# Another order for the attention steps and for the end of the last chunk in a one-core attention and expert kernel

## The chip, the cores and the metric

The kernel runs on one core of a Trainium2 chip. The core has a matrix engine (TensorE: PE for its matmuls, PEld for its weight loads), a vector engine (VectorE, DVE), a scalar engine (ScalarE, ACT), a general engine (GpSimd, POOL) and an engine that here only issues DMAs (SyncE, SP). Each of them takes its instructions strictly in the order in which they were written. They meet through semaphores. The metric is the device time of one execution in microseconds; lower is better.

## The reference

Three parts follow each other. The first is attention for 4 batches and 8 heads over 512 local and 32 global positions: local queries see the global keys and a band of keys at a distance of at most 32, global queries see everything.

```python
s_ll = np.where(np.abs(pos[:, None] - pos[None, :]) <= 32, s_ll, -1e9)
out_l = np.matmul(sm(np.concatenate([s_lg, s_ll], -1)), np.concatenate([v_g, v_l], 2))
out_g = np.matmul(sm(scale * np.matmul(q_g, k_all.transpose(0, 1, 3, 2))), v_all)
```

Its 2176 token rows of 512 go to 8 experts. `logits = x @ w_gate` are sorted over all tokens and experts, and each token goes to the expert of its largest logit that still has room (272 places each). Each expert computes `relu(x @ w1[e]) @ w2[e]` with 1024 hidden columns. The third part is dense: `h = x @ w_in` with 2048 hidden columns, a rational function `g = P(h) / (Q(|h|) + 1e-6)` of each element, and `g @ w_out`. Everything is computed in an accuracy close to float32; a product in the later parts is therefore three matmuls on high and low parts.

## The kernel before, in words

**The order is written by a planner.** Every piece of work is a Python generator that yields what it needs: an engine and a modelled duration (`yield "PE", 0.36`), an event, a buffer of a ring, or a float, which is a delay. `Flow.run` (L165 and on) asks which step could start first by the modelled clocks and writes that step's instructions next. The durations decide only the order; on the chip the semaphores decide the time. There are two planners: one for attention, one for all that follows.

**Attention.** A unit is 128 queries of one batch, all heads: 16 units, with a unit for the global queries of each batch between them. For a unit, PE computes scores (L589 adds the mask, L599 the products), VectorE takes the extreme of each row (`mx`, L614), ScalarE the exponentials (`A`, L299), PE transposes them (L632), PE multiplies by the values (`av`, L655), VectorE scales by the sums (`rs`, L663 and L664; `xs`, L666). SP then stores `xs` to DRAM, PE transposes it (L684), ScalarE or VectorE copies it (`XT`, L299), PE multiplies by the gate (L699), a copy goes to `lgT`, PE adds four quarters (L708) and VectorE copies 8 columns to `LG` (L710). These last five steps are `logits`. Before the units of a batch, keys are turned (`kr` to `KT`: PE L493, copies L299 or L306) and queries as well (`qr` to `QB`: L513, L299 or L308). Whole rows of keys and values for the windows are put together by DMAs (`VW<-vr`) and by copies of the global values on GpSimd (`VW<-vg`, L465). A copy marked `CPY` goes to ScalarE or VectorE, as the planner finds.

Beside that, 24 of 32 pieces of the third part's weights come in as 64-bit numbers in `stg` buffers (6 of them) and are turned into float32: one operation on ScalarE (L277) and three on VectorE (L278, L279, L280).

**Routing and experts.** When the last `LG` is there, a search on VectorE (L999 and on) finds the rows of the first expert; later searches lie beside matmuls. Experts run one after the other (L1250 to L1252).

**The third part** runs in 8 chunks of token blocks of 128: seven chunks of two blocks and the last one of three. `firsts` is the first layer (L1250 to L1252, into a `tq` bank, of which there are 2), `chain` the rational function on ScalarE and VectorE (L1626 to L1666; the step L1638 gives the bank back), `seconds` the second layer (L1255 to L1257, into one bank for each block). The last chunk has 16 steps. A step is 12 matmuls of the first layer and 9 of the second, 3 for each block. `store` copies a finished block on ScalarE (L1709) and scatters its rows by an indirect DMA from GpSimd (L1714). Which of `firsts` and `seconds` goes first is a matter of ranks: `seconds` has the lower rank, by 0.1, until `firsts` has reached the last chunk (`front["d"] >= E - 1`), and a higher one from there.

Of the kernel before, what the change touches and what calls it, by code (L numbers as in the profile page):

```python
# [2 lines left out]

# [28 lines left out]
FL, FM, SR = 0.45, 0.7, 0.1  # L32
WT = 5
PATIENCE = {"DVE": 0.3, "PE": 0.15, "ACT": 0.2, "POOL": 0.5}
NL = 8
LGPAD, RCPAD = 96, 160
LAG = 0.5
LAND = (5.0, 3.3, 2.3)
DRAWN = (4.5, 4.0, 3.0)


REBIAS = 2.0 ** -112
# [2 lines left out]
class Event:  # L45


    def __init__(self, n=1):
        self.n, self.at, self.waiters, self.ring = n, [], [], None
# [27 lines left out]
class Flow:  # L77
# [5 lines left out]

    SAME = {"PE": 0.0, "DVE": 0.14, "ACT": 0.08, "POOL": 0.1}

    def __init__(self, fill=None):
        self.clock, self.asks, self.now, self.fill = {}, [], [(0.0, "PE")], fill

    def lag(self, src, dst):
        return self.SAME.get(src, 0.0) if src == dst else 0.2  # L90
# [80 lines left out]
    def run(self, patience):  # L171
        while self.asks:
            best = {}
            for p in self.asks:
                r = p[1]() if callable(p[1]) else p[1]
                t, e, d = min((max([self.free(e)] + [t + self.lag(s, e) for t, s in p[2]]) + sum(less), e, d)
                              for e, d, *less in p[3])
                best.setdefault(e, []).append((t - (e == "DVE" and len(p[3]) > 1) * BIAS, r, p, d))
            pick = None
            for e, c in best.items():  # L180
                t0 = min(x[0] for x in c)
                wait = patience.get(e, 0.0)
                wait = wait() if callable(wait) else wait
                x = min((x for x in c if x[0] <= t0 + wait), key=lambda x: (x[1], x[0]))
                if pick is None or x[0] < pick[0]:
                    pick, self.engine = x, e
            t, _, p, d = pick
            e = self.engine
            if e == "PE" and self.fill is not None:
                self.fill(t - self.clock.get(e, 0.0))  # L190
            self.asks.remove(p)
            self.clock[e] = t + d
            p[2] = [(t + d, e)]
            self._on(p)
# [7 lines left out]
def moe_kernel(ctx: ExitStack, tc: tile.TileContext, q_l, k_l, v_l, q_g, k_g, v_g, w_gate, w1, w2,  # L202
# [81 lines left out]
    with ExitStack() as actx:  # L284
# [6 lines left out]

        ORD = [2 * (hh % 4) + hh // 4 for hh in range(H)]
        kraw, qraw, vraw, vgr = {}, {}, {}, {}
        flow = Flow()
        V = nc.vector
        CPY = [("ACT", 0.48), ("DVE", 0.6, BIAS)]

# [341 lines left out]
        def values(b, u, rank, at, sm, m, turned):  # L639
            yield turned  # L640
            yield vw_in[b, u // 2]
            if rank:
                yield valued[rank - 1]
            av = yield av_s
            flow.fire(valued[rank])
            pv = bank("av", 1)
            for n in range(4):
                yield "PE", 0.38
                w = win(4 * u + n)
                vw = VW[b, w // (NW // 2)][:, w % (NW // 2)]  # L650
                for hg in range(2):
                    c0 = (2 * n + hg) * D
                    for j in range(4):
                        h = ORD[4 * hg + j]
                        nc.tensor.matmul(pv[32 * j:32 * j + 32, c0:c0 + D], at[0][:, hg, n, 32 * j:32 * j + 32],  # L655
                                         vw[:, h * D:(h + 1) * D], start=True, stop=True)
            flow.fire(at[1])
            flow.fire(vw_used[b, u // 2])
            x = yield xs_s
            xs = work.tile([128, 4, 2 * D], F32, name="xs", bufs=2)  # L660
            yield "DVE", 0.2
            rs = few.tile([128, 8], F32, name="rs", bufs=3)
            V.tensor_scalar(rs, sm.rearrange("p a b -> p (a b)"), 1e-9, None, op0=OP.add)  # L663
            V.reciprocal(rs, rs)  # L664
            yield "DVE", 0.6
            V.tensor_tensor(xs.rearrange("p n (a d) -> p (n a) d", a=2), pv.rearrange("p (a d) -> p a d", d=D),  # L666
                            rs[:, :, None].to_broadcast([128, 8, D]), op=OP.mult)
            flow.fire(av)
            flow.fire(m)
            xs_free = Event(5)  # L670
            flow.go(after(xs_free, x), 0)

            def stores():
                for j in range(4):
                    yield "SP", 0.475
                    dma(dram(xd, (b * S + SG + u * 128) * DM + j * 128, [[DM, W], [W * DM, 4], [1, 128]]),
                        xs[32 * j:32 * j + 32], xs_free, 0.267)

            flow.go(stores(), rank + ST)
            tx = yield tx_s  # L680
            px = bank("tx", 1)
            yield "PE", 0.5
            for n in range(4):
                nc.tensor.transpose(px[:, n * 128:(n + 1) * 128], xs[:, n], identf)  # L684
            flow.fire(xs_free)
            xt = yield xt_s
            XT = work.tile([128, KC, 128], F32, name="XT", bufs=2)
            yield CPY
            copy(XT.rearrange("p j (n q) -> p n j q", n=4), px.rearrange("p (n j q) -> p n j q", n=4, j=4))
            flow.fire(tx)  # L690
            yield from logits(XT, 4 * b + u)
            flow.fire(xt)

        def logits(XT, c):
            tx = yield tx_s
            p = bank("tx", 1)
            yield "PE", 0.36
            for j in range(KC):
                nc.tensor.matmul(p[32 * j:32 * j + 32, :128], wg[:, j], XT[:, j], start=True, stop=True)  # L699
            yield [("ACT", 0.2), ("DVE", 0.2, BIAS)]  # L700
            lgT = work.tile([128, 128], F32, name="lgT", bufs=2)
            copy(lgT, p[:, :128])
            flow.fire(tx)

            tx = yield tx_s
            p = bank("tx", 1)
            yield "PE", 0.3
            tail_pe[:] = [nc.tensor.matmul(p[:, :E], lgT, sel, start=True, stop=True)]  # L708
            yield "DVE", 0.08
            V.tensor_copy(LG[:, c], p[:, :E])  # L710
            flow.fire(tx)
# [960 lines left out]
    def seconds():  # L1672
        for c in range(E):
            T, FW = shape(c)
            ng = T // 128
            for i in range(NSTEP[c]):
                yield g_done[c][i]
                gh, gl, slots = gs.pop((c, i))
                if i == 0:
# [4 lines left out]
                for w in range(FW):  # L1684
# [3 lines left out]
                    for g in range(ng):  # L1688
# [5 lines left out]
                        if f == FFC - 1:  # L1694
                            flow.go(store(c, g), 0.7)
                flow.fire(slots)

    ixs = {}

# [42 lines left out]
    with tc.manual_schedule(engines={ET.PE, ET.Activation, ET.DVE, ET.Pool}), tc.issue_after(tail[-1].ins), tc.issue_after(tail_pe[0].ins):  # L1742
        for gen, rank in ((router(), pace), (high(), 5), (last_pieces(), late), (low_pe(), 5), (low(V, "DVE", 0.6), late), (gather(), 0.5), (loads(), 1), (splits(), 1.5),
                          (experts(), lambda: 2 + front["e"]), (firsts(), lambda: 2 + front["d"]),
                          (seconds(), lambda: 2 + front["d"] + (SR if front["d"] >= E - 1 else -0.1))):
            flow.go(gen, rank)
        flow.run({**PATIENCE, "PE": lambda: PATIENCE["PE"] if xs_ else 0.55})

# [30 lines left out]
```

## Time and profile before

| | us |
|---|---|
| median of 3 runs | 876.4 |
| lowest of the 3 | 875.96 |
| highest of the 3 | 2771.55 |
| the profiled execution | 868.81 |
| its span, first to last instruction | 867.0 |

1.8 us of the profiled execution lie around its span. It is 7.6 us shorter than the median. The page gives busy times, the chain of work that ended last, and groups of instructions; the trace behind it can be asked for a stretch, an engine or a line. Times in it are counted from the span's start. An instruction's row has its start, its length, and in brackets the idle time of its engine before it with what ended that. Attention lies between 0 and 180 us, the first routing between 180 and 237, experts and chunks between 237 and 786, and from 786 on the last chunk is computed.

### The profile page before, as it was taken

What the parts mean: (1) busy time and instruction counts of PE and PEld (TensorE: products, weight loads), DVE (VectorE), ACT (ScalarE), POOL (GpSimd) and SP (SyncE); (2) the same over time, 40 slices, a digit from 0 to 9 for tenths busy, and PEclk for the clock granted to TensorE, in tenths of its full rate; (3) what the DMA queues carried; (4) which work ended last, traced back from release to release, by engine and by line L of the source; (5) the groups of instructions that cost most, each with busy time, mean ns of one, the idle gap of its engine ahead of it and who ended that gap; (6) DMA issues with size and microseconds to landing.
All of it is one profiled execution on the core that took longest, in us unless ns stands there. A gap on an engine that the chain in (4) does not pass through costs nothing.

```text
span 867.0 us, 21692 instructions
## 1 busy us (share of the span) xinstructions
PE 815.3 (94%) x8532; PEld 715.9 (83%) x8532; DVE 709.6 (82%) x1647; ACT 500.1 (58%) x1135; POOL 254.8 (29%) x223
## 2 busy tenths in 40 slices
PE   8988777889799999999999999999999999999997
PEld 5765555667599899989989999999999999998995
DVE  3577677688789999989989989999886867668985
ACT  5777485788355446644554564554465555555763
POOL 5511111000252323424233442424344243330001
PEclk9999897899899999999999999999999999999999
DMA  9989897234452212321321232132123132300000
GB/s 236 252 217 283 223 281 223 90 98 125 132 151 83 62 48 64 108 72 42 96 87 49 62 98 74 50 94 90 50 63 111 48 97 68 93 26 13 12 1 38
DMA packets 130543, 89.08 MB, mean 103 GB/s; under 512 B 28840, under 2 KB 119464, under 8 KB 130440
## 3 DMA queue, kind: packets, MB, share of 16 engines
q1 hardware_dynamic: 126632, 76.92, 30.9%
q0 software_dynamic: 3280, 10.75, 3.8%
q8 instruction: 67, 1.10, 0.5%
q14 instruction: 36, 0.29, 0.1%
q10 hardware_dynamic: 528, 0.02, 0.0%
HBM read 70.02 MB, written 8.92 MB: 91 GB/s over the span
## 4 chain that ended last, share of the span: by engine, by line
PE 65%; DVE 14%; issue 10%; ACT 5%; DMA 2%; POOL 2%; SPq 1%; DVEq 0%; POOLq 0%; ACTq 0%
PE sc L1250 6%; PE sc L1252 6%; PE sc L1251 6%; PE tq L1250 6%; PE tq L1251 6%; PE tq L1252 6%; PE sc L1257 5%; PE sc L1255 5%; PE sc L1256 5%; PE av L1025 2%; SPq L393 1%; PE sc L599 1%; PE av L655 1%; DVE wide_a L1021 1%; PE tq L632 1%
## 5 line engine op out<-in xcount | busy, mean ns | idle before, releaser
L1495 POOL TENSOR_TENSOR wlo<-rows,whi 128x512 fp32r<-128x512 f32 x120 | 167.6, 1399 | 333.0 <-ACT whi L1486 324.0
L1250 PE MATMUL tq<-yr,wh 128*128 128x256 f32 (+1 forms) x512 | 148.9, 291 | 1.5 <-DVE p L1638 1.5
L1252 PE MATMUL tq<-yr,ws 128*128 128x256 f32 (+1 forms) x512 | 148.0, 289 | 0.0
L1251 PE MATMUL tq<-yr,wh 128*128 128x256 f32 (+1 forms) x512 | 147.9, 289 | 0.0
L1250 PEld LDWEIGHTS tq<-yr,wh 128*128 128x128 f32 x512 | 96.9, 189 | 3.3 <-issue 2.2
L1255 PE MATMUL sc<-wh,t 128*128 128x512 f32 x248 | 99.4, 401 | 0.0
L1257 PE MATMUL sc<-wh,t 128*128 128x512 f32 x248 | 98.4, 397 | 0.8 <-DVE t L1666 0.8
L1251 PEld LDWEIGHTS tq<-yr,wh 128*128 128x128 f32 x512 | 97.0, 189 | 0.8
L1256 PE MATMUL sc<-ws,t 128*128 128x512 f32 x248 | 97.3, 392 | 0.0
L1252 PEld LDWEIGHTS tq<-yr,ws 128*128 128x128 f32 x512 | 97.0, 189 | 0.0
L1486 ACT ACTIVATE whi<-rows 128x512 fp32r<-128x512 f32 x120 | 75.0, 628 | 16.5 <-PE sc L1251 12.9
L1530 ACT ACTIVATE hh<-sc 128x272 fp32r<-128x272 f32 x64 | 25.4, 396 | 87.0 <-PE sc L1252 86.7
L1626 ACT ACTIVATE t<-tq,coef 128x512 f32<-128x512 f32 (+1 forms) x67 | 44.8, 668 | 52.2 <-PE tq L1252 40.7
L1250 PE MATMUL sc<-xhi,whi 128*128 128x272 f32 x240 | 73.5, 306 | 0.0
L1250 PE MATMUL sc<-hh,whi 128*128 128x272 f32 x240 | 70.8, 295 | 0.0
L1252 PE MATMUL sc<-xhi,wlo 128*128 128x272 f32 x240 | 69.9, 291 | 0.5 <-POOL wlo L1495 0.3
L1251 PE MATMUL sc<-xlo,whi 128*128 128x272 f32 x240 | 69.6, 290 | 0.0
L1251 PE MATMUL sc<-hl,whi 128*128 128x272 f32 x240 | 69.6, 290 | 0.0
L1252 PE MATMUL sc<-hh,wlo 128*128 128x272 f32 x240 | 69.3, 289 | 0.0
L1644 DVE SCALAR_TENSOR_TENSOR t<-t,b 128x512 f32<-128x512 f32 (+1 forms) x67 | 52.1, 778 | 20.1 <-ACT t L1628 19.9
L1647 ACT ACTIVATE t<-t,cq 128x512 f32<-128x512 f32 (+1 forms) x67 | 47.3, 706 | 23.4 <-DVE t L1644 23.0
L1257 PEld LDWEIGHTS sc<-wh,t 128*128 128x128 f32 x248 | 46.6, 188 | 15.0 <-DVE t L1666 4.8
(307 smaller groups left out, 2143.1 us busy)
## 6 DMA issues: line engine op xcount, KB each, us to landing
rows<-in_moe_w_dram SPq DMA_DIRECT2D x128, 256.0 KB, 2.8
stg<-in_moe_w_in_dram SPq DMA_DIRECT2D x16, 512.0 KB, 4.0
stg<-in_moe_w_out_dram SPq DMA_DIRECT2D x16, 512.0 KB, 6.6
VW<-vr SPq DMA_DIRECT2D x18, 256.0 KB, 6.2
kr<-in_k_l_dram SPq DMA_DIRECT2D x8, 512.0 KB, 5.7
qr<-in_q_l_dram SPq DMA_DIRECT2D x8, 512.0 KB
vr<-in_v_l_dram SPq DMA_DIRECT2D x16, 256.0 KB, 4.7
xd<-xs SPq DMA_DIRECT2D x64, 64.0 KB, 3.5
```

What stands on the lines that cost most here:

```text
L1250: nc.tensor.matmul(ps, whi, xhi, start=first, stop=False)
L1251: nc.tensor.matmul(ps, whi, xlo, start=False, stop=False)
L1252: nc.tensor.matmul(ps, wlo, xhi, start=False, stop=last)
L1255: nc.tensor.matmul(ps, ghi, whi, start=first, stop=False)
L1256: nc.tensor.matmul(ps, ghi, wlo, start=False, stop=False)
L1257: nc.tensor.matmul(ps, glo, whi, start=False, stop=last)
L1486: nc.scalar.activation(hi, raw, AF.Copy)
L1495: (V if alt else nc.gpsimd).tensor_tensor(lo, raw, hi.bitcast(F32), op=OP.subtract)
L1530: nc.scalar.activation(hh, ph[:, :CAP], AF.Relu)
L1626: nc.scalar.activation(q, ph, AF.Abs, scale=b0)
L1644: V.scalar_tensor_tensor(q, r, b1, q, op0=OP.mult, op1=OP.add)
L1647: nc.scalar.activation(r, q, AF.Ln, bias=cq)
```

## The change

Four things are altered.

- In the attention planner each modelled duration is multiplied by a number between 0.97 and 1.03, drawn from a generator with a fixed seed (31). The order is thus a fixed one again, but another.
- `logits` yields a delay of 0.7 us, in the model only, ahead of each of its three requests, for all units but those of the last three ranks. It does this ahead of taking a `tx` bank.
- `seconds` takes the higher rank already from `front["d"] >= E - 1.2`, which is within the last chunk but one.
- The last two steps of the last chunk's second layer are written block by block: both steps of block 0 and its store, then block 1, then block 2. Before, all blocks of step 14 came ahead of those of step 15.

No instruction is added or taken away. Three copies into `KT` go from ScalarE to VectorE (one from `kgT`, two from `sc`); that is the only change in the numbers of instructions on an engine.

```diff
+VARY = (31, 0.03)
+SLACK = 0.7
-    def __init__(self, fill=None):
-        self.clock, self.asks, self.now, self.fill = {}, [], [(0.0, "PE")], fill
+    def __init__(self, fill=None, vary=None):
+        self.clock, self.asks, self.now, self.fill, self.vary = {}, [], [(0.0, "PE")], fill, vary
...
             self.asks.remove(p)
+            if self.vary is not None:
+                d *= 1 + self.vary.uniform(-VARY[1], VARY[1])
             self.clock[e] = t + d
...
-        flow = Flow()
+        flow = Flow(vary=random.Random(VARY[0]))
...
-            yield from logits(XT, 4 * b + u)
+            yield from logits(XT, 4 * b + u, SLACK * (rank < 5 * B - 3))
             flow.fire(xt)
 
-        def logits(XT, c):
+        def logits(XT, c, late=0.0):
+            yield late
             tx = yield tx_s
             p = bank("tx", 1)
             yield "PE", 0.36
...
+            yield late
             tx = yield tx_s
             p = bank("tx", 1)
             yield "PE", 0.3
             tail_pe[:] = [nc.tensor.matmul(p[:, :E], lgT, sel, start=True, stop=True)]
+            yield late
             yield "DVE", 0.08
...
-            for i in range(NSTEP[c]):
+            pair = NSTEP[c] - 2 * (c == E - 1)
+            for i in range(pair):
...
+            if pair == NSTEP[c]:
+                continue
+            both = []
+            for i in (pair, pair + 1):
+                yield g_done[c][i]
+                both.append((i, *gs.pop((c, i))))
+            for g in range(ng):
+                o = slice(g * 128, g * 128 + 128)
+                for f, gh, gl, _ in both:
+                    yield "PE", mmt(512, 3)
+                    mm3t(accs[c][g], gh[:, o], gl[:, o], *wo(f), False, f == FFC - 1)
+                flow.go(store(c, g), 0.7)
+            for x in both:
+                flow.fire(x[3])
...
-                          (seconds(), lambda: 2 + front["d"] + (SR if front["d"] >= E - 1 else -0.1))):
+                          (seconds(), lambda: 2 + front["d"] + (SR if front["d"] >= E - 1.2 else -0.1))):
```

Lines of the changed kernel are 5 to 8 higher in attention and 8 higher in the chunks (L666 is L671 there, L710 is L718, L1257 is L1265). Between the end of attention and the last steps of the last chunk but one, every engine's order is the same as before. Three places follow.

The first is VectorE in the third batch of attention, at 91 us of the trace. `stg_1372` and the like are pieces of weights; `av` and `xs` belong to a unit, `mx` to the next one. Before:

```order
L710 COPY LG<-tx 128x8
L614 TENSOR_REDUCE mx<-sc 128x4 x2
L663 TENSOR_SCALAR rs<-sm 128x8
L664 RECIPROCAL rs<-rs 128x8
L279 SCALAR_TENSOR_TENSOR ws<-stg_1372,ws 128x512
L666 TENSOR_TENSOR xs<-av,rs 128x512
L280 SCALAR_TENSOR_TENSOR ws<-stg_1372,ws 128x512
L306 COPY KT<-sc 128x4x4x32 x2
```

Now:

```order
L619 TENSOR_REDUCE mx<-sc 128x4 x2
L668 TENSOR_SCALAR rs<-sm 128x8
L669 RECIPROCAL rs<-rs 128x8
L671 TENSOR_TENSOR xs<-av,rs 128x512
L718 COPY LG<-tx 128x8
L311 COPY KT<-sc 128x4x4x32
L283 TENSOR_SCALAR ws<-stg_1561 128x512
L284 SCALAR_TENSOR_TENSOR ws<-stg_1561,ws 128x512
L285 SCALAR_TENSOR_TENSOR ws<-stg_1561,ws 128x512
L311 COPY KT<-sc 128x4x4x32
```

The copy of logits and the piece's operation no longer stand ahead of `xs`; the pieces have moved behind it.

The second is VectorE at the end of attention, down to the last two copies of logits, small set-up operations of the routing apart. Of the two `LG` in each piece the first is the last unit's but one, the second the last unit's; the global queries' `LG` stands ahead of what is shown. Before:

```order
L279 SCALAR_TENSOR_TENSOR ws<-stg_2712,ws 128x512
L278 TENSOR_SCALAR ws<-stg_2725 128x512
L663 TENSOR_SCALAR rs<-sm 128x8
L664 RECIPROCAL rs<-rs 128x8
L710 COPY LG<-tx 128x8
L666 TENSOR_TENSOR xs<-av,rs 128x512
L280 SCALAR_TENSOR_TENSOR ws<-stg_2712,ws 128x512
L279 SCALAR_TENSOR_TENSOR ws<-stg_2725,ws 128x512
L280 SCALAR_TENSOR_TENSOR ws<-stg_2725,ws 128x512
L710 COPY LG<-tx 128x8
```

Now:

```order
L285 SCALAR_TENSOR_TENSOR ws<-stg_2705,ws 128x512
L284 SCALAR_TENSOR_TENSOR ws<-stg_2713,ws 128x512
L283 TENSOR_SCALAR ws<-stg_2759 128x512
L285 SCALAR_TENSOR_TENSOR ws<-stg_2713,ws 128x512
L718 COPY LG<-tx 128x8
L284 SCALAR_TENSOR_TENSOR ws<-stg_2759,ws 128x512
L668 TENSOR_SCALAR rs<-sm 128x8
L669 RECIPROCAL rs<-rs 128x8
L285 SCALAR_TENSOR_TENSOR ws<-stg_2759,ws 128x512
L671 TENSOR_TENSOR xs<-av,rs 128x512
L718 COPY LG<-tx 128x8
```

Ahead of these rows stand the `LG` of the global queries and three operations of the last pieces. All three operations of every piece now stand ahead of the last `xs`; before, three of them came behind it.

The third is PE at the very end (`wh_4121` are the weights of step 14, `wh_4769` those of step 15). Before, each step's three matmuls stand three times, once for each block, and the end of it reads:

```order
L1255 MATMUL sc<-wh_4121,whi 128x512
L1256 MATMUL sc<-ws,whi 128x512
L1257 MATMUL sc<-wh_4121,wlo 128x512
L1255 MATMUL sc<-wh_4769,t_12339 128x512
L1256 MATMUL sc<-ws,t_12339 128x512
L1257 MATMUL sc<-wh_4769,t_12339 128x512
```

Now the two alternate, block by block, to the end:

```order
L1263 MATMUL sc<-wh_4121,whi 128x512
L1264 MATMUL sc<-ws,whi 128x512
L1265 MATMUL sc<-wh_4121,wlo 128x512
L1263 MATMUL sc<-wh_4769,t_12338 128x512
L1264 MATMUL sc<-ws,t_12338 128x512
L1265 MATMUL sc<-wh_4769,t_12338 128x512
L1263 MATMUL sc<-wh_4121,whi 128x512
```

Block 0 has its sum after 6 of the last 18 matmuls, block 1 after 12, block 2 after 18; before it was 12, 15 and 18. Earlier in the same chunk each of its first eleven first-layer steps stands 3 to 12 matmuls of the second layer further ahead than before, or level.

## Rows read from the trace of the kernel before

**Rows 1.** The page's first line.
```profile
span 867.0 us, 21692 instructions
```
**Rows 2.** Busy time by stage: stretch, its length, each engine's busy time, clock, DMA.
```profile
0.00:180.00 180.00, 146.73 (x3282) 105.06 (x3283) 123.01 (x382) 118.78 (x421) 40.73 (x45) 0.92 0.78 220
237.00:786.00 549.00, 544.92 (x4420) 506.07 (x4419) 475.85 (x986) 294.88 (x550) 203.16 (x164) 1.00 0.25 74
786.00:867.00 81.00, 73.35 (x367) 65.36 (x366) 64.76 (x121) 46.83 (x90) 5.42 (x9) 0.99 0.04 17
```
**Rows 3.** The page's chain that ended last, by engine.
```profile
PE 65%; DVE 14%; issue 10%; ACT 5%; DMA 2%; POOL 2%; SPq 1%; DVEq 0%; POOLq 0%; ACTq 0%
```
**Rows 4.** Waits from 20 to 166 us: who waited for whom, us, times, longest.
```profile
PE tx L699 <- ACT XT L299: 2.1, 3, 0.7
PE tx L708 <- ACT lgT L299: 1.0, 2, 0.5
```
**Rows 5.** Timeline, 91 to 103 us, of VectorE, GpSimd and PE.
```profile
91.45 3.40 POOL L465 COPY VW<-vg 32x2048 f32<-32x2048 f32 x2 [16.58 <-issue]
92.32 1.05 DVE L663 TENSOR_SCALAR rs<-sm 128x8 f32<-128x8 f32 x1
93.52 1.88 DVE L279 SCALAR_TENSOR_TENSOR ws<-stg,ws 128x512 int32<-128x512 int32 x1
95.32 0.68 DVE L666 TENSOR_TENSOR xs<-av,rs 128x512 f32<-128x512 f32 x1
96.08 1.97 PE L493 MATMUL sc<-identf,kr 128*64 128x128 f32 x16 [3.75 <-DVE xs L666]
102.44 0.17 DVE L710 COPY LG<-tx 128x8 f32<-128x8 f32 x1 [3.66 <-PE tx L708]
```
**Rows 6.** Busy time by stretch, as Rows 2, right behind that gap.
```profile
95.00:100.00 5.00, 3.92 (x28) 3.29 (x32) 2.89 (x5) 0.61 (x2) 0.00 (x0) 0.50 0.90 205
```
**Rows 7.** VectorE in 0 to 180 us by line: busy, mean ns; idle before.
```profile
L279 DVE SCALAR_TENSOR_TENSOR ws<-stg,ws 128x512 int32<-128x512 int32 x24 | 18.8, 784 | 4.4 <-ACT stg L277 3.5
L280 DVE SCALAR_TENSOR_TENSOR ws<-stg,ws 128x512 int32<-128x512 int32 x24 | 16.5, 689 | 0.3
L278 DVE TENSOR_SCALAR ws<-stg 128x512 int32<-128x512 int32 x24 | 11.2, 467 | 1.6 <-DMA stg<-in_moe_w_out_dram 1.6
L306 DVE COPY KT<-sc 128x512 f32<-128x512 f32 x7 | 4.8, 687 | 1.5 <-PE sc L493 1.5
L306 DVE COPY KT<-kgT 128x896 f32<-128x896 f32 x3 | 1.9, 621 | 3.3 <-ACT kgT L299 3.3
```
**Rows 8.** Timeline of VectorE at the end of attention.
```profile
171.34 0.17 DVE L710 COPY LG<-tx 128x8 f32<-128x8 f32 x1 [3.30 <-PE tx L708]
176.88 0.69 DVE L666 TENSOR_TENSOR xs<-av,rs 128x512 f32<-128x512 f32 x1
```
**Rows 9.** Timeline of the last chunk's first steps.
```profile
795.43 0.58 ACT L1626 ACTIVATE t<-tq,coef 128x384 f32<-128x384 f32 x1 [2.72 <-DVE t L1666]
800.33 0.41 PE L1250 MATMUL tq<-yr,wh 128*128 128x384 f32 x1 [1.54 <-DVE p L1638]
```
**Rows 10.** Timeline of the end.
```profile
856.08 0.56 DVE L1666 TENSOR_TENSOR t<-t 128x384 fp32r<-128x384 f32 x1
856.65 0.39 PE L1255 MATMUL sc<-wh,whi 128*128 128x512 f32 x1
858.69 0.39 PE L1255 MATMUL sc<-wh,t 128*128 128x512 f32 x1
859.57 1.96 ACT L1709 ACTIVATE rows<-sc 128x512 f32<-128x512 f32 x3 [7.08 <-PE sc L1257]
860.44 0.96 POOL L1714 DMA_INDIRECT out_dram<-rows,ix  x1 [54.17 <-ACT rows L1709]
860.50 0.39 PE L1257 MATMUL sc<-wh,t 128*128 128x512 f32 x1
862.97 0.96 POOL L1714 DMA_INDIRECT out_dram<-rows,ix  x1 [0.22 <-issue]
```

More of the change, by code (lines that the diff above doesn't have):

```diff
@@ L1 @@
 import math
+import random
 from contextlib import ExitStack
```

## The prediction

> **What bounds the kernel now.** I read the views from the coarse to the fine. First comes the busy time by stage [rows 2]: from 237 to 786 us PE works 544.92 of 549.00 us, so nothing on another engine can be worth anything there, and the order there is the same in both kernels but for its last few us. In attention PE works 146.73 of 180.00 us, at a mean granted clock of 0.92, and VectorE 123.01: no engine is full, and PE loses 33 us to waits and some more to the clock. In the last chunk PE works 73.35 of 81.00 us. Then comes the chain of waits [rows 3]: PE carries 65% of it and VectorE 14%. PE's engine is thus the one whose delays mostly count, and a delay on VectorE counts where PE waits for it. The waits by releaser [rows 4] and the timelines [rows 5, 8 to 10] give the sizes.
>
> The sum is made against the profiled execution: a span of 867.0 us [rows 1] and 1.8 us around it, 868.8 us. The median of the three runs, 876.4 us, is 7.6 us above that. I work out a difference and take it from the median.
>
> **A. The end, block by block.** The last 18 matmuls stand 0.227 us apart: nine of them lie between 856.65 and 858.69 [rows 10]. Before, block 0 is full after the 12th, which ends at 856.65 + 11 x 0.227 + 0.39 = 859.54, and indeed its copy starts at 859.57. The three copies of 0.65 us each follow without a gap, but the stores on GpSimd go out at 860.44 and twice 1.26 us later (the last at 862.97), so the last store stands behind two others and not behind its copy. Now block 0 is full after the 6th (858.2) and block 1 after the 12th, where block 0 was. Their stores go out at about 859.1 and 860.44. Block 2 is full after the 18th, as before: 860.50 + 0.39 = 860.9, its copy ends at 861.5, and with the 0.22 us from a copy's end (859.57 + 0.65) to its store (860.44) the last one goes out at 861.8 against 862.97. That is **-1.2 us**. Two things could spoil it. The matmuls of step 15 are needed sooner: the 4th of the 18 rather than the 10th, thus at 857.33, and VectorE's last operation for them ends at 856.08 + 0.56 = 856.64, so 0.7 us of cover remain. And GpSimd is free from 860.44 + 0.96 = 861.40, in time. The bounds are -1.4 (the store behind the copy without a gap) and 0 (that cover gone).
>
> **B. The last chunk's first layer sooner.** PE waits 1.54 us at 800.33 for a `tq` bank that the chain on VectorE gives back (L1638); that chain stood behind ScalarE's 795.43 activation, for which 2.72 us of idle time ended with a VectorE operation [rows 9]. In the new order the first layer's steps stand 3 to 12 matmuls of the second layer further ahead, so the chain's work is asked for sooner. At the step that waited, it is three matmuls, 3 x 0.227 = 0.68 us, and the operation that frees its bank stands behind a chain that began about 1.5 us sooner. The wait may vanish (-1.54), or PE asks 0.68 us sooner for a bank that comes no sooner, and the wait grows to 2.2 us, with the matmuls that could have filled it now behind it (+0.7). I take the middle of the case for it, half of the wait: **-0.8 us**. It is not nearer to the end, since the two orders differ in what ScalarE has ahead of the chain as well.
>
> **C. Logits asked for later.** Nothing is issued more or less; in the order, PE's gate products and quarter sums and the small copy on VectorE stand further back, with other matmuls ahead of them. What PE loses to them between 20 and 166 us are two groups of waits: 2.1 us for `XT` and 1.0 for `lgT` [rows 4]. With 0.7 us of other work ahead of each request, and the longest wait 0.7, all of these can go: 3.1 us at most. PE has 65% of the chain [rows 3], so 3.1 x 0.65 = 2.0: **-2.0 us**. The bounds are -3.1 and 0. Who is late next is nobody on the path: `LG` is not used until the routing begins, and the last three ranks have no delay.
>
> **D. The stall at 92 us.** PE stands still for 3.75 us until 96.08, for `xs` [rows 5]. Ahead of `xs` on VectorE stands a piece's operation that takes 1.88 us against a mean of 0.784 [rows 5, 7], while GpSimd copies global values (91.45 to 94.85); and ahead of the scaling stood an `LG`. In the new order `xs` comes first, the `LG` and the pieces behind it. `xs` could then start where that operation did, at 93.52: 1.8 us sooner. Behind the stall the granted clock is 0.50 (1.2 instead of 2.4 GHz) over the 5 us from 95 [rows 6], which costs up to 2.5 us more: PE's 3.92 busy us there hold what takes half as long at 2.4 GHz, and the first turns of keys take 1.97 us. A PE that had not stood still before might keep its clock. Gap and clock are 3.75 + 2.5 = 6.3 us. That all of it goes is one end, that the new order has a like stall beside it the other, 0. I take half, **-3.1 us**: the 1.8 us that are plain in the order and half of the clock's 2.5. The moved pieces are hidden as long as VectorE has its 57 idle us in attention (180 less 123.01); uncovered, each costs its 0.7 to 0.8.
>
> The row of the 1.88 us operation bears on one page. The Trainium skill's "SBUF — State Buffer", section "Who interferes with whom", says that a VectorE instruction with two SBUF inputs contends with a GpSimd instruction that reads SBUF, and that whichever comes first holds the shared ports for the whole instruction. This trace agrees: such an operation took 1.1 us more while GpSimd copied. By that rule the moved pieces only collide with another copy, and D would be smaller; that is the third rival.
>
> **E. The end of attention.** The last `xs` starts at 176.88 [rows 8] and the routing's search needs its `LG`, so this place is on the path wholly. Before, six operations of the last three pieces lie between the global queries' `LG` (171.34) and it, and three behind it; now all nine stand ahead, of 0.47, 0.78 and 0.69 us by kind [rows 7]. The three that changed sides (two of L280, one of L279) are 2.2 us by these means; idle time of VectorE before 176.88, and the last unit's `av`, which is not there much sooner, cover two thirds: `xs` starts at about 177.6. **+0.7 us**; bounds 0 and +2.2.
>
> **F. Copies into `KT` on VectorE.** One from `kgT` (0.62 us) and two from `sc` (0.69 each) [rows 7] move from ScalarE: 2.0 us more on VectorE, as much less on ScalarE, both with idle time in this stage (118.78 busy on ScalarE). PE waits for keys as for `xs`. I take a third, **+0.7 us**, between 0 (hidden) and +2.0 (all on the path): near the lower end, as VectorE has 14% of the chain.
>
> SP has one piece's transfer more between the stores of the last units; DMA engines are 78% busy in attention [rows 2] and the store's reader is the routing behind, so I cost this at nothing. Other places, where an `xs` comes a little sooner or later, I take as even: also nothing.
>
> The sum is -1.2 - 0.8 - 2.0 - 3.1 + 0.7 + 0.7 = -5.7 us: 863.1 against the profiled 868.8, and **870.7 against the median**.
>
> **The rivals.** *Attention stays as long as it was.* Its matmuls are the same, and a stall that is taken from one unit turns up at another, as buffers and weights' transfers set a pace that no order changes. For it speaks that DMA is 78% busy; against it, that the long stall has a plain cause in the order. Then A and B remain: -2.0, 874.4 us.
>
> *The clock.* A granted clock of 0.92 over 180 us, with levels 1 and 0.5, means 16% of it, 28.8 us, at 1.2 GHz, and a loss of up to 14.4 us if PE is busy in all of it. If the new order has fewer stalls, half of this goes beyond D: 14.4 x 0.65 x 0.5 = 4.7 us. That gives -10.4, 866.0 us. Against it speaks that nothing in the change aims at PE's stalls in general.
>
> *Collisions.* The moved pieces lie under GpSimd's copies (40.73 us busy in attention [rows 2]) at two places on the path, 1.1 us each: D is -0.9, the sum -3.5, 872.9 us. The page's rule above would have it so.
>
> *Slower: VectorE becomes the one for whom PE waits.* The three copies count fully (+2.0), the last `xs` is late (+0.7), and a new wait for a copy or an `xs` brings one more stretch of 5 us at half clock (+2.5) where C and D give nothing; A and B give back 2.0. That is +3.2, **879.6 us**. It decides from the point on where the pieces and copies that now stand ahead of an `xs` or `KT` take longer than the unit's `av` on PE. For it: at 92 us such a thing happened with a single operation. Against it: 57 us of idle time on VectorE.
>
> **How the numbers follow.** Forecast 0.52, attention unchanged 0.18, collisions 0.08, clock 0.09, slower 0.13. The good ends of A to D together are -1.4 - 1.5 - 3.1 - 6.3 = -12.3, 864.1 us; with a quarter of the clock's 4.7 on top it is about 863.0, the low end. The high end is the slower rival, 879.6; B's bad end, E's and F's lie inside it. What lies outside are the far parts of the clock's case and of the slower one, and cases not thought of. 2%, about what a measurement of this kernel can tell from no change, is 17.5 us: no case as priced here reaches it. Several stalls gone or come at once could: of the clock's 0.09 I give that 0.04, for faster, and of the slower case's 0.13 I give it 0.03; 0.93 lies within.
>
> **What would show it.** A: the last store at about 861.8 less the shift, 0.9 us behind the last matmul's end, and stores no longer 1.26 us apart. B: no wait of PE for L1638's successor around 800 us, or a smaller one. C: PE's waits for `XT` and `lgT` between 20 and 166 us gone. D: no PE gap of 3 us and no stretch at 0.50 behind it near 95 us, with `xs` ahead of the pieces. E: the last `xs` later against the end of PE's `av`. F: PE's waits for `KT` from VectorE not over 1 us more. The prediction is wrong if attention ends later than 180 us, if the mean clock there falls below 0.92, or if the experts' stage shifts by more than 1 us.

## The result, and the profile after

The changed kernel took 860.44 us (median of 6 runs, 856.58 to 861.78), the kernel before 875.87 us beside it (median of 6, one of them 2771.55). The two medians lie 15.4 us apart; the ratio, which is used from here on, is 0.9863, with an interval from 0.983 to 0.9895: **12.0 us less, between 9.2 and 14.9**. Run once more, in an experiment below, it was 0.9885 (0.9858 to 0.9913), 10.0 us less. It is faster, by less than 2% and by about twice the forecast of 5.7 us; 0.9863 of 876.4 us is 864.4 us, near the low end of the range that was given.

The page's first line and chain answer to [rows 1, 3]. PE's share of the chain rose by one point and DMA's by two; ScalarE's fell by three.

```profile
span 858.2 us, 21675 instructions
...
PE 66%; DVE 14%; issue 10%; DMA 4%; ACT 2%; POOL 2%; SPq 1%; POOLq 0%; DVEq 0%; ACTq 0%
```

The span is 8.8 us shorter. Where they went is read from stages that are cut at the same instruction. The cut is the second operation of the routing's first search, at 175.72 us instead of 180.82 ("first search" from here on); here is busy time by stage, cut there, behind the routing and at the last chunk, which answers to [rows 2]:

```profile
0.00:175.72 175.72, 147.11 (x3277) 105.52 (x3285) 121.30 (x387) 117.47 (x419) 40.36 (x45) 0.92 0.82 226
175.72:231.00 55.28, 49.59 (x470) 38.79 (x469) 46.32 (x162) 39.53 (x75) 5.54 (x5) 0.93 0.41 129
231.00:779.50 548.50, 544.59 (x4422) 506.39 (x4421) 475.56 (x983) 296.84 (x552) 204.04 (x164) 1.00 0.25 75
779.50:858.20 78.70, 73.02 (x360) 64.81 (x359) 64.11 (x120) 45.57 (x87) 5.19 (x9) 0.99 0.04 17
```

The kernel before, cut at its own first search:

```profile
0.00:180.82 180.82, 147.55 (x3284) 105.79 (x3285) 123.48 (x385) 118.80 (x422) 40.73 (x45) 0.92 0.78 219
```

PE is busy for the same time in attention, at the same mean clock; what is gone is 4.7 us of its standing still (33.3 to 28.6). The routing, from the first search to the first gather on GpSimd (219.13 before, 213.12 now), takes 37.4 us instead of 38.3; it takes 38.7 and 39.0 in the two other profiles of the new order, so that is not the order's. From there to 700 us GpSimd's indirect DMAs come 5.8 to 6.4 us sooner, so the experts' stage did not move. The last matmul starts 7.7 us sooner (860.50 to 852.80), the last store 8.9 us.

The waits of PE from 20 to 200 us (waiting engine, tile and line, what ended the wait: us, times, longest), before:

```profile
PE tx L684 <- DVE xs L666: 8.2, 7, 2.8
PE tq L766 <- ACT Ag L299: 4.5, 2, 2.5
PE sc L493 <- DVE xs L666: 3.8, 1, 3.8
PE tx L823 <- DVE xsg L811: 3.5, 4, 1.5
PE tx L699 <- ACT XT L299: 3.1, 5, 0.7
PE tx L708 <- ACT lgT L299: 1.7, 4, 0.5
...
PE tx L684 <- DVE LG L710: 0.4, 1, 0.4
```

and in the changed kernel:

```profile
PE tx L689 <- DVE xs L671: 4.5, 3, 2.1
PE tx L831 <- DVE xsg L819: 4.2, 4, 2.8
PE av L660 <- ACT AT L304: 2.7, 1, 2.7
PE tx L689 <- DVE LG L718: 2.6, 2, 1.3
PE tx L705 <- ACT XT L304: 2.0, 4, 0.7
...
PE sc L498 <- DMA kr<-in_k_l_dram: 1.5, 2, 1.0
PE tq L774 <- ACT Ag L304: 1.4, 1, 1.4
...
PE tx L715 <- ACT lgT L304: 0.9, 2, 0.5
```

Over all its rows that view sums to 31.6 us before and 25.9 now. The waits that went are those for `xs` (8.2 + 3.8 to 4.5) and for `Ag`, the exponentials of the global queries (4.5 to 1.4), of which the forecast had nothing. Waits that grew are those for `xsg`, the global queries' `xs` (3.5 to 4.2), the one for `LG` (0.4 to 2.6), and one for `AT`, the turned exponentials (0.6 to 2.7); the last is 0.8 in the two other profiles of this order.

The place of the stall [rows 5], now, on VectorE, GpSimd and PE:

```profile
92.15 3.41 POOL L470 COPY VW<-vg 32x2048 f32<-32x2048 f32 x2 [18.88 <-issue]
92.38 1.69 DVE L668 TENSOR_SCALAR rs<-sm 128x8 f32<-128x8 f32 x1
94.10 0.20 DVE L669 RECIPROCAL rs<-rs 128x8 f32<-128x8 f32 x1
94.40 0.69 DVE L671 TENSOR_TENSOR xs<-av,rs 128x512 f32<-128x512 f32 x1
95.22 0.66 PE L689 MATMUL tx<-identf,xs 128*128 128x128 f32 x4 [1.29 <-DVE LG L718]
96.84 0.88 PE L498 MATMUL sc<-identf,kr 128*64 128x128 f32 x12 [0.97 <-DMA kr<-in_k_l_dram]
```

The 3.75 us gap is gone; two of 1.29 and 0.97 are there. The first ends with the `LG` copy that now stands behind `xs`. An operation beside GpSimd's copy is still long: the small `rs` (1.69 us, 1.05 before, 0.16 or 0.17 where no copy runs), while the piece's operations are now behind the copy.

Where the longest wait for `Ag` ended before, at 113.58, ScalarE had other work ahead of it:

```profile
108.24 0.21 DVE L750 TENSOR_SCALAR nmg<-m 128x1 f32<-128x1 f32 x1
109.90 1.26 ACT L277 ACTIVATE stg<-stg 128x512 f32<-128x512 f32 x2
111.19 1.28 ACT L299 ACTIVATE QB<-sc 64x512 f32<-64x512 f32 x2
112.48 0.69 ACT L299 ACTIVATE Ag<-sc,nmg 128x512 f32<-128x512 f32 x1
113.58 0.66 PE L766 MATMUL tq<-identf,Ag 128*128 128x128 f32 x4 [2.52 <-ACT Ag L299]
```

The same place in the changed kernel:

```profile
103.64 0.21 DVE L758 TENSOR_SCALAR nmg<-m 128x1 f32<-128x1 f32 x1
105.22 0.71 ACT L304 ACTIVATE Ag<-sc,nmg 128x512 f32<-128x512 f32 x1
106.78 0.63 PE L774 MATMUL tq<-identf,Ag 128*128 128x128 f32 x4
```

From the end of `nmg`, an input of `Ag`, to the start of `Ag` it was 4.0 us, with two pieces and two copies of queries among what ScalarE did between; now it is 1.4, and PE does not wait. No run changed ScalarE's order here alone, so how much of the gain hangs on this wait is not shown.

The end of attention [rows 8] and the wait ahead of its last transposes (VectorE, PE):

```profile
170.04 0.16 DVE L718 COPY LG<-tx 128x8 f32<-128x8 f32 x1
171.59 0.68 DVE L671 TENSOR_TENSOR xs<-av,rs 128x512 f32<-128x512 f32 x1
172.33 0.66 PE L689 MATMUL tx<-identf,xs 128*128 128x128 f32 x4 [2.09 <-DVE xs L671]
175.19 0.17 DVE L718 COPY LG<-tx 128x8 f32<-128x8 f32 x1 [2.91 <-PE tx L715]
```

PE's wait for the last `xs` grew from 0.99 to 2.09 us. The last chunk's wait [rows 9] and the end [rows 10]:

```profile
797.53 0.41 PE L1258 MATMUL tq<-yr,wh 128*128 128x384 f32 x1 [0.67 <-DVE p L1646]
...
850.51 0.60 ACT L1732 ACTIVATE rows<-sc 128x512 f32<-128x512 f32 x1 [7.18 <-PE sc L1265]
851.38 0.96 POOL L1737 DMA_INDIRECT out_dram<-rows,ix  x1 [53.52 <-ACT rows L1732]
852.75 0.96 POOL L1737 DMA_INDIRECT out_dram<-rows,ix  x1 [0.31 <-ACT rows L1732]
852.80 0.39 PE L1265 MATMUL sc<-wh,t 128*128 128x512 f32 x1
853.23 0.60 ACT L1732 ACTIVATE rows<-sc 128x512 f32<-128x512 f32 x1 [0.76 <-PE sc L1265]
854.10 0.96 POOL L1737 DMA_INDIRECT out_dram<-rows,ix  x1 [0.31 <-ACT rows L1732]
```

Each store goes out behind its own copy. The last one starts 1.30 us behind the start of the last matmul; it was 2.47.

### The profile page after: what moved, and what is told of

Its sections match the earlier page's. It is cut to its first block, busy times and chain, and to the rows that moved or that the text cites. A ratio compares the mean times of both kernels' runs of the same rounds, so it can differ in the third digit from the quotient of the medians.

```text
span 858.2 us, 21675 instructions
## 1 busy us (share of the span) xinstructions
PE 814.3 (95%) x8525; PEld 715.5 (83%) x8532; DVE 707.3 (82%) x1650; ACT 499.4 (58%) x1132; POOL 255.1 (30%) x223
## 4 chain that ended last, share of the span: by engine, by line
PE 66%; DVE 14%; issue 10%; DMA 4%; ACT 2%; POOL 2%; SPq 1%; POOLq 0%; DVEq 0%; ACTq 0%
PE sc L1258 7%; PE sc L1260 6%; PE sc L1259 6%; PE tq L1258 6%; PE tq L1259 6%; PE tq L1260 6%; PE sc L1265 6%; PE sc L1263 6%; PE sc L1264 5%; PE av L1033 2%; PE tq L1369 2%; PE sc L604 1%; DVE wide_a L1029 1%; POOL VW L455 1%; DMA VW<-vr 1%
## 5 line engine op out<-in xcount | busy, mean ns | idle before, releaser
L1265 PE MATMUL sc<-wh,t 128*128 128x512 f32 x248 | 98.3, 396 | 0.8 <-DVE t L1674 0.8
L1265 PEld LDWEIGHTS sc<-wh,t 128*128 128x128 f32 x248 | 46.5, 188 | 14.9 <-DVE t L1674 4.7
```

The source lines that it names most:

```text
L1265: nc.tensor.matmul(ps, glo, whi, start=False, stop=last)
```

## The experiments

Each was timed against the kernel before on the same chip. The table has them all; the clock is the mean of the granted clocks of the timed runs, and behind the stroke that of the kernel before beside it. The first search and PE's waits (sum of the view of waits, 20 to 200 us) come from one profile each. "Less" in us is the ratio times the median of the kernel before beside it.

| kernel | time against before, interval | clock / before's | first search, us | PE's waits, us |
|---|---|---|---|---|
| before | 1 | | 180.8 | 31.6 |
| the change | 0.9863 (0.983 to 0.9895) | 0.980 | 175.7 | 25.9 |
| the change again | 0.9885 (0.9858 to 0.9913) | 0.975 / 0.972 | 178.4 | 27.4 |
| e1, end alone | 0.9985 (0.9953 to 1.0017) | 0.972 / 0.974 | 185.9 | 33.8 |
| e2, first layer alone | 0.9959 (0.9928 to 0.999) | 0.975 / 0.974 | 181.3 | 32.7 |
| e3, draw alone | 0.9963 (0.9935 to 0.9991) | 0.976 / 0.974 | 183.0 | 32.2 |
| e4, delay alone | 1.0006 (0.9971 to 1.0042) | 0.972 / 0.974 | 190.5 | 33.6 |
| e5, draw and delay | 0.9868 (0.9833 to 0.9904) | 0.978 / 0.973 | 172.1 | 24.8 |
| e6, seed 1 | 1.001 (0.9984 to 1.0036) | 0.971 / 0.973 | 188.6 | 34.7 |
| e6, seed 2 | 0.9936 (0.9902 to 0.997) | 0.977 / 0.973 | 180.6 | 34.1 |
| e6, seed 3 | 0.986 (0.9815 to 0.9904) | 0.982 / 0.973 | 175.8 | 26.7 |
| e9, 42 matmuls more | 1.0031 (1.0009 to 1.0053) | 0.980 / 0.972 | 185.3 | 26.8 |
| e10, 24 matmuls more | 0.997 (0.9926 to 1.0013) | 0.979 / 0.975 | 178.1 | 25.9 |
| e11, the change and 28 more | 0.9889 (0.9855 to 0.9923) | 0.983 / 0.975 | 177.3 | 26.4 |

**e1, the end alone.** The loop over the last chunk's steps stops two short, and the last two are written block by block, as in the change:

```diff
-            for i in range(NSTEP[c]):
+            pair = NSTEP[c] - 2 * (c == E - 1)
+            for i in range(pair):
...
+            for g in range(ng):
+                for f, gh, gl, _ in both:
+                    mm3t(accs[c][g], gh[:, o], gl[:, o], *wo(f), False, f == FFC - 1)
+                flow.go(store(c, g), 0.7)
```

> The kernel before with the end block by block and nothing else. Theory (term A): stores behind each other were the end, so the last store starts about 0.9 us behind the end of the last matmul instead of 2.1, in the profile; everything before is as it was. Time -1.2 us (0.9986 of before). Rival: the landing of the last store, not its issue, ends the run, and the three landings overlap less now: 0 to -0.5 us. In the timed runs both lie near the noise; the profile's rows of the end decide.

The last store starts 1.30 us behind the start of the last matmul, against 2.47 or 2.48 in all seven profiles with the old end; in all seven with the new one it is 1.30. That is 1.17 us. The span from that store to the end stays at 4.0 to 4.1 us, so the rival falls. In the timed runs (1.3 us less, between 4.1 less and 1.5 more) it can't be told from nothing, as expected. What was not expected is that attention, whose order is that of before, took 185.9 us here.

**e2, the first layer alone.**

```diff
-(SR if front["d"] >= E - 1 else -0.1)
+(SR if front["d"] >= E - 1.2 else -0.1)
```

> The kernel before with the first layer of the last chunk sooner and nothing else. Theory (term B): PE's wait for the tq bank in the last chunk falls from 1.5 us to 0.7 or less, and the last matmul comes about 0.9 us sooner against the first search of the routing: -0.9 us. Rival: the shift of 1 us seen in the changed kernel there is a difference between two executions and not the order: 0, with the 1.5 us wait still there.

PE's wait for the `tq` bank is 0.8 us instead of 1.5. From the first gather to the last matmul it is 639.9 us here and 641.4 before. Over seven profiles with the old rank the mean is 641.4 (640.4 to 642.0), over seven with the new one 640.7 (639.7 to 641.5). The sooner first layer is thus worth about 0.7 us, with a spread as wide as that. The wait itself is 0.5 to 1.0 us in the seven, but in three of them it comes twice (1.2 to 1.6 us in all). The timed runs gave 3.6 us less (0.9 to 6.3), more than this; in its profile attention ends where it did (181.3 us), so where the rest comes from is not shown.

**e3, the draw alone**, and **e4, the delay alone.**

```diff
+VARY = (31, 0.03)
...
+            if self.vary is not None:
+                d *= 1 + self.vary.uniform(-VARY[1], VARY[1])
```

> The kernel before with the drawn durations in attention and no delay of the logits. Theory (the forecast's terms C to F): what counts is that logits stand behind other work, so the draw alone gives little: attention's end (first search of the routing) within 1.5 us of before's 180.8, the stall near 92 us of about 3.7 us still there. Rival (a draw is a lottery ticket): the order as such moves things, and the draw alone takes 3 us or more away.

```diff
+            yield from logits(XT, 4 * b + u, SLACK * (rank < 5 * B - 3))
...
+            yield late
             tx = yield tx_s
```

> The kernel before with the logits asked for 0.7 us later and no draw. Theory (C and D): the stall near 92 us is gone, the waits for XT and lgT are shorter, and the first search begins at 176 to 178 us instead of 180.8: -3 to -5 us. Rival (lottery): the delay without the draw that fits it moves the stalls elsewhere, and the end of attention is within 1.5 us of 180.8, or later.

The draw alone gave 3.2 us (0.8 to 5.7), which does not tell the theory from the rival. In its profile the first search comes 2.2 us later than before (183.0), and near 92 us a gap of 3.2 us is left, ended by a transfer of keys, so no gain shows there. The delay alone gave nothing, and in its profile (of a run of 877.7 us, where the median was 872.9) the first search comes at 190.5 instead of 176 to 178. The waits of PE there:

```profile
PE tx L685 <- DVE xs L667: 8.1, 5, 3.7
PE tq L770 <- ACT Ag L300: 4.6, 2, 3.2
...
PE tx L685 <- DVE LG L714: 3.2, 1, 3.2
```

All waits for `XT` fell from 3.3 to 2.0 us, as forecast. But there is one `tx` bank, and a request that is made later gives it back later: PE waited 3.2 us for it until an `LG` copy, at 98.9 us, near the place of the old stall, where all such waits before were 0.4. `XT`, `lgT` and `LG` together are 5.4 us before, 6.5 here and 6.3 in the changed kernel. The theory of e4 fell.

**e5, draw and delay, ends as before.**

```diff
+VARY = (31, 0.03)
+SLACK = 0.7
```

> The kernel before with draw and delay in attention, its end and its first layer as before. Theory (the parts add up): the whole change less what the end (1.2 us) and the sooner first layer (1.5 us in the profile) gave: -15 + 2.7, about -9 to -12 us against before's median, where the draw alone gave -2.4 and the delay alone +0.6; thus draw and delay together are not the sum of the two. Mean granted clock of its runs near 0.980, where before's are near 0.973. Rival: most of the changed kernel's gain was the chip and the day of its six runs: -2 to -5 us, clocks as before's.

11.5 us less (8.4 to 14.6), where the draw alone gave 3.2 less and the delay alone 0.5 more. The two don't add up: together they are a third order. Nearly the whole gain of the change is in attention.

**e6, other seeds**, 1, 2 and 3, with all else as in the change:

```diff
-VARY = (31, 0.03)
+VARY = (1, 0.03)
```

> The changed kernel with seed 1 in place of 31. Theory (lottery): every draw is another order, and the gain goes with the order and the clock it gets, not with the delay: somewhere between -12 and +5 us. Rival (the delay needs any draw): within 3 us of the changed kernel.

> The changed kernel with seed 2. As for seed 1: by the lottery between -12 and +5 us, the three seeds at least 5 us apart from each other; by the rival within 3 us of the changed kernel.

> The changed kernel with seed 3. As for seeds 1 and 2. If time follows the mean granted clock over all these kernels as it does over the runs of before (7.5 us for 0.01), the slower seeds show lower clocks.

Seed 1 is 0.9 us slower than before (1.4 less to 3.1 more, so no change is not excluded), seed 2 5.6 faster, seed 3 12.2 faster. Each has the ends' gain of some 2 us in it. The same delay and the same size of draw thus give anything from nothing to the whole gain. The slower seeds have the lower clocks, as expected (0.971, 0.977, 0.982). No single wait decides: seed 3 has the whole gain with 4.0 us of waits for `Ag`, and seed 2 is faster with more waits (34.1) than the kernel before (31.6), as PE is busy for 2.1 us less in attention (145.5). Attention of seed 1, which answers to the rows of stages above:

```profile
0.00:188.62 188.62, 150.74 (x3277) 108.61 (x3285) 124.44 (x388) 117.99 (x420) 40.91 (x45) 0.90 0.75 210
```

PE is idle for 37.9 us there, 9.3 more than in the changed kernel, and busy for 3.6 more, at a lower clock.

**e9, PE kept busy.** In the runs of the kernel before, the time follows the mean granted clock: over the 35 runs beside e1 to e4 it is 7.5 us for 0.01, with a correlation of -0.89 (864.7 us at 0.985, 878.5 at 0.971); over those of the three other chips it is 6.8 to 7.6. Whether the clock is the cause was tried with matmuls of ones, ahead of transposes for which PE waits in that order.

```diff
+        def busy(p, kind):
+            for _ in range(BUSY.get((kind, seen[kind]), 0)):
+                nc.tensor.matmul(p.rearrange("p (a b) -> p a b", a=4), onesb,
+                                 onesb[:, None, :].to_broadcast([128, 4, 128]), start=True, stop=True)
+            seen[kind] += 1
...
             yield "PE", 0.5
+            busy(px, "xs")
```

> The kernel before with 42 more matmuls (ones, 128x512, results overwritten) at six places in attention where PE stood still in all three profiles of that order: ahead of the transposes of xs (3rd, 11th, 12th, 16th unit) and of Ag (3rd, 5th), as many as fit into the wait (about 9 us of PE work in all). Nothing waits for them but PE's next instruction. Theory (the clock falls because PE stands still in these places): mean granted clock of the runs 0.977 or more against 0.973, time -2 to -5 us. Rival 1 (the clock follows from how much PE works, not from its standing still): clock the same or lower, time 0 to +4 us. Rival 2 (clock has nothing to do with either): clock as before, time 0 to +1 us.

The clock rose from 0.972 to 0.980, and the time rose as well, by 2.7 us; none of the three expectations fits in both. Three rows (PE) show how the edit missed a part of its aim:

```profile
67.74 1.89 PE L699 MATMUL tq<-onesb 128*128 128x512 bf16 x8 [1.92 <-ACT Ag L299]
...
136.02 2.75 PE L699 MATMUL tx<-onesb 128*128 128x512 bf16 x12
139.10 0.66 PE L685 MATMUL tx<-identf,xs 128*128 128x128 f32 x4 [0.34 <-DVE xs L666]
```

Those ahead of `xs` fill the wait, of which 0.34 us is left here. The 18 ahead of `Ag` stand behind the wait, as the `tq` bank itself comes free with `Ag`, and cost 5.3 us on top (1.89 and 3.37).

**The change again**, unaltered, beside e9:

> The changed kernel once more, on one chip with the kernel before, for a second profile of its order. Theory: PE's waits in attention are fewer in this order in every execution (25 to 27 us from 20 to 200 us against 31.6 to 34 in three profiles of the order before), and the clock of its runs is higher (near 0.980); ratio 0.984 to 0.988. Rival: the short waits are those of one lucky execution; then this profile shows 30 us or more and the ratio is 0.99 or above.

The short waits are the order's and not one execution's: 27.4 us here, 25.9 and 24.8 in the two other profiles of it (the change and e5), against 31.6, 33.8 and 32.7 for the order before (before, e1 and e2). The wait for `Ag` is 1.4 or 1.5 us in each of the three, 4.5 to 5.3 in the three of the order before. The clock did not come out as expected: 0.975, not 0.980. Attention in the other profiles of the two orders, up to the first search: the old order in e1 and e2, then the new one here and in e5.

```profile
0.00:185.89 185.89, 149.64 (x3284) 106.87 (x3285) 122.70 (x384) 118.95 (x423) 40.63 (x45) 0.91 0.76 213
0.00:181.28 181.28, 146.76 (x3284) 104.91 (x3285) 123.76 (x384) 118.67 (x422) 40.54 (x45) 0.93 0.79 219
0.00:178.37 178.37, 149.99 (x3284) 108.11 (x3285) 121.95 (x388) 116.74 (x420) 40.49 (x45) 0.90 0.79 222
0.00:172.14 172.14, 145.91 (x3277) 105.59 (x3285) 121.16 (x387) 116.86 (x419) 40.66 (x45) 0.94 0.83 230
```

With the two rows of the result that makes three of each. PE stands still for 33.3, 36.3 and 34.5 us in the old order and 28.6, 28.4 and 26.2 in the new one, a mean of 6.9 us less; it is busy for 148.0 and 147.7 us on average, and the clock averages 0.92 in both. In the profiles the gain in attention is thus PE's standing still, and not its clock.

**e10, only the 24 ahead of `xs`**, and **e11, 28 in the changed kernel** (4 and 5 ahead of the 3rd and 13th unit's transposes, 8 ahead of the last, 11 ahead of the last `xsg`).

```diff
+        BUSY = {("xs", 2): 4, ("xs", 10): 12, ("xs", 11): 4, ("xs", 15): 4}
```

> The kernel before with only the 24 extra matmuls ahead of the transposes of xs, which in the run with 42 filled waits of PE (the other 18 stood behind a wait for Ag and cost 5.3 us there). Theory (a PE that stands still loses clock, and the clock is worth 7.5 us for each 0.01): clock 0.976 or more against 0.973, time -2 to -3 us. Rival (the clock is raised by more work alone and gives nothing back): clock up, time 0 to +1 us.

```diff
+        BUSY = {("xs", 2): 4, ("xs", 12): 5, ("xs", 15): 8, ("xsg", 3): 11}
```

> The changed kernel with 28 extra matmuls at four places where its PE waits for xs or xsg in all three profiles of its order (0.75 to 2.8 us each). Theory: clock up by 0.002 to 0.004, time 1 to 3 us below the changed kernel, ratio to the kernel before 0.982 to 0.986. Rival: ratio as the changed kernel's, 0.986 to 0.989, or worse by what the last ones delay.

e10: clock 0.979 against 0.975, 2.6 us less, with an interval (6.5 less to 1.1 more) that takes in both the theory and no change. e11: clock 0.983 against 0.975, and no faster than the change without it. The clock rose with more matmuls at these places, clearly in e9 (by 0.007, over 12 runs with a standard deviation of 0.004) and less surely in e10 (by 0.004, standard deviation 0.005). That clock won back in this way pays is not shown: e10's 2.6 us are near what 0.004 would be worth by the 7.5 us for 0.01, but its interval takes in nothing as well. The version with 28 more does not beat the change.

## Why the prediction was right, and where its sizes were off

The direction and the range held: 864.4 us against 863.0 to 879.6. That the result lies at the low end of the range and still inside it is in part luck, since that end was added up from the good ends of A to D and some of the clock, while much of the gain came from waits of which the sum had no term. Measured on each term:

**A, the end: right.** -1.2 forecast, -1.17 in the profiles, by the mechanism named.

**B, the first layer: right in size.** -0.8 forecast, about -0.7 measured; one wait of 1.5 us became one or two of 0.5 to 1.0, between the two bounds.

**C, the logits: wrong.** -2.0 forecast on the step that the waits for `XT` and `lgT` "can go" and that who is late next "is nobody on the path". Late next is the single `tx` bank: the waits moved to `LG`, and the three together went from 5.4 us to 6.3. Worth 0 or a little less than nothing, where the bounds were -3.1 and 0.

**D, the stall at 92 us: the gap and the 1.8 us right, the clock open.** The gap of 3.75 us went, against two smaller ones. `xs` did not start at 93.52, as `rs` ahead of it took 1.69 us, but the unit's step from the `xs` before it to its own is 7.7 us (86.68 to 94.40) where it was 9.1. Over the three profiles of each order the steps are 9.1, 9.1 and 9.8 before and 7.7, 7.7 and 7.3 now, 1.7 us less on average. The other half of the term hung on the clock behind the gap. With the order of before and a gap of 3.21 us at the same place, e2 had a granted clock of 1.00 there (against 0.50 in [rows 6]); in e1 the gap of 2.86 us ended at 99.49, and the clock behind it was 0.66. First e2, then e1:

```profile
95.00:100.00 5.00, 3.89 (x52) 3.14 (x53) 3.11 (x5) 2.23 (x8) 0.17 (x1) 1.00 0.81 185
100.00:105.00 5.00, 4.75 (x38) 3.50 (x36) 1.40 (x4) 2.91 (x9) 0.00 (x0) 0.66 0.86 247
```

In the three profiles of the new order both stretches are at 1.00. The dip thus came behind this gap in two of three executions, and a single profile can't price it. The rival "collisions" was there, at its place, with a small price: `rs` took 1.69 us beside the copy in the changed kernel's first profile and 1.32 in e5, and 0.16 in the profile of the repeat, where the copy began behind it. By the Trainium skill's "SBUF — State Buffer", section "Who interferes with whom", a single-source VectorE operation contends with GpSimd only in a mode that uses both ports; that `rs` is in one is not shown here, that it is long beside the copy is.

**E, the end of attention: right, and a little small.** +0.7 forecast, PE's wait for the last `xs` +1.1 (0.99 to 2.09); it is 2.11 and 2.36 in the other two profiles of the new order. **F** can't be told apart; no wait of PE for `KT` from VectorE shows.

**What was missing** is the wait for `Ag`, 3.1 us, and a part of those for `xs` beyond the stall: ahead of the 11th unit's transposes, at 132 us, 2.84 (2.98 in the two other profiles), in the new order 0.6 or none. I read the order of VectorE and PE at three places and not that of ScalarE, which set this wait. In the sum: attention took 180.8, 185.9 and 181.3 us in three profiles of the old order, 175.7, 178.4 and 172.1 of the new one, means 182.7 and 175.4: -7.3, where C to F were -3.7. PE's standing still is 6.9 of it. With A and B it is -9.2, at the edge of the first interval and within the second.

The rival "the clock" gave 866.0 us, nearer to 864.4 than the forecast, but not by its mechanism: the clock in attention averages 0.92 over the three profiles of either order. It is 0.92, 0.90 and 0.94 in the new one, so the sign of being wrong that was set at "below 0.92" is finer than the spread.

The sum was also made against a profile that stood at the fast end of its kernel: 868.8 us, where 35 later runs have a mean of 872.2. The 5 to 6 us by which attention differs between two profiles of one order are more than any term of the sum. In the timed runs the clock is a part of the gain. The clocks of the same attention order are higher than those beside them by 0.003 in the repeat and 0.005 in e5; by the 7.5 us for 0.01 that would be 2 of 10.0 and 4 of 11.5 us. An estimated 7 to 8 us thus remain at an equal clock, about what PE's shorter waits are in the profiles. Whether the shorter waits raised the clock is not shown; waits and clock go together, and e9 to e11 did not part them.

## What to carry to other kernels

A delay that is put ahead of a request for a single buffer moves the wait to the next holder; count the buffer's whole round before booking the wait as gone. When an order is drawn anew, read every engine's queue ahead of each long wait of the bounding engine, ScalarE's too, and expect draws of one kind to differ by more than the reason given for them: here four seeds lay between +0.9 and -12.2 us. One profile of a stage with many short waits has a spread of its own (here 5 to 6 us in 180), so a term smaller than that needs several profiles or a row that is the same in all of them.

## What the runs showed of the hardware

In the 94 runs beside the experiments, on four chips, the time of the kernel before lay between 861.4 us (at a mean granted clock of 0.987) and 878.5 us (at 0.971), a wider span than the gain of the change, and on each chip it followed the mean granted clock (6.8 to 7.6 us for 0.01). In the profile of the changed kernel the dips lie in attention and the first routing (0.92 and 0.93), as the stage from 231 us on has 1.00 and the last chunk 0.99. A dip of one profile need not come back: behind the same gap in the same order the clock was 0.50, 0.66 and 1.00. Another 24 and 42 matmuls at places where PE waits raised the mean clock by 0.004 and 0.007.
